# Attention and a rational-activation feed-forward on one core: new first loads, w_in laid out by chunk, and the weights' high parts rounded on GpSimd

## The chip, the cores and the metric

The kernel runs on 1 core of a Trainium2 chip. The metric is the device time of one execution in microseconds (us). Engines are named as the profile names them: PE (TensorE; PEld is its weight load), DVE (VectorE), ACT (ScalarE), POOL (GpSimd), SP (SyncE, which here only issues DMAs).

## The reference

Eight batches of eight heads, 576 positions of 64. Each head has a softmax attention over positions pooled by 4 and one over the 3 neighbours on either side; their sum is the input of a feed-forward layer with a rational function in the middle. The weights come as 64-bit floats (`float32 * (1.0 / np.sqrt(...))`).

```python
q_d, k_d, v_d = mean over groups of 4 positions of q, k, v
out_up    = np.repeat(sm_attn(q_d, k_d, v_d), 4, axis=2)
out_local = softmax(where(|i - j| < 4, q k^T / 8, -1e9)) @ v
x = (out_up + out_local).transpose(0, 2, 1, 3).reshape(4608, 512)

h = x @ w_in                       # 512 x 2048
P = a[0] + a[1] * h + a[2] * h**2 + a[3] * h**3
Q = 1.0 + abs(b[0]) * abs(h) + abs(b[1]) * h**2
return (P / (Q + 1e-06)) @ w_out   # 2048 x 512
```

## The kernel before

**Blocks.** The 4608 rows of x are worked in blocks of 512 rows (the first 512 positions of a batch), and in two blocks that hold the 64 remaining positions of four batches. The 2048 hidden columns are 16 chunks of 128 (`NFC`). For a block and a chunk, `h_part` makes h in PSUM, `middle` computes the rational function on ACT (four or five L710 operations per step) and DVE (L725 to L743, seven operations) into a high part `g` and a residue, and `o_part` (L762) multiplies with that chunk of w_out and adds up in four PSUM banks over all chunks. PE multiplies rounded pairs: high times high, low times high, high times low. In the first block alone `h_part` takes the unrounded weight and x in full precision (L685, two PE records per product) instead of the pairs (L697), so that the residues of w_in are needed only by the second block.

**Weights.** `weights(w, f, spot)` brings chunk f of w_in (w = 0) or w_out (w = 1) to SBUF. SP loads 512 KB of 64-bit words into a staging spot (L311 for w_in, L316 for w_out); ACT rescales the upper words (L325); DVE shifts them and puts the two words together as a 32-bit float `wb` (L328, L331). `parts` then rounds it to the high part `wh` (L345, on ACT) and subtracts for the residue `wl` (L348, on DVE). `wl` has the place of `wb`. The spots are called `st0` to `st4`, `sl0` to `sl3`, `sx0`, `sx1`; some lie in the room of later tiles. A load is 128 rows for w_out and 4 x 128 runs of 256 words for w_in, whose rows are 2048 columns long.

**Attention.** Work goes by pairs of heads, four pairs a batch, two pairs at a time. For a pair: `scores` (PE, L404 mask and L414), `softmax_local` (maximum on DVE, L446 and L453, exponentials on ACT, L461), the same for the pooled scores (`scores_pooled` L431, `softmax_pooled` L476 to L487), `normalize` (DVE L498 to L522), `turned` (transposes on PE, L535 and L542, copied back by ACT as `ept` and `et`, L548 to L559; the banks are its second argument), `weighted` (PE: the pooled part L584, which wants `vf` or `vp`, and the local part L573; ACT makes `up`, L630; DVE adds both into x, `xf`, L616). The pooled v of batch 0 is `vf`: one SP load (L816) and three accumulating DMAs that POOL issues (L820), each after the one before has landed. For later batches `pq` and `vp` are made likewise (L377 on SP, L381 on POOL).

**Order.** All instructions are first recorded as tasks with an engine, a cost and, for some, a due time. `Plan.run` goes through time and gives each free engine the ready task with the earliest latest-start; the result is a fixed order on each engine, and at run time the engines wait only for semaphores. A due time or a cost thus moves instructions. In the gaps of PE's planned order before the first block, products that nothing reads (`warm`, L898) are put in. Every engine works its order through one by one, so whatever waits holds up all that is behind it on that engine.

Of the kernel before, what the change touches and what calls it, by code (L numbers as in the profile page):

```python
# [9 lines left out]
F32 = mybir.dt.float32  # L10
# [9 lines left out]
DM, DF = 512, 2048  # L20
P = 128
NPAIR = H // 2
NCC = DM // P
NFC = DF // P
POOL = 4
# [51 lines left out]
class Plan:  # L77
# [11 lines left out]
    def add(self, engine, dur, fn, reads=(), writes=(), due=None, lag=None):  # L89
        t = Task()  # L90
        t.engine, t.dur, t.fn, t.due, t.n = engine, dur, fn, due, len(self.tasks)
        t.lag, t.preds, t.succs, t.late, t.start = lag, {}, [], 1e9, None
        rk = set().union(*(r.keys for r in reads)) if reads else set()
        wk = set().union(*(w.keys for w in writes)) if writes else set()
        for k in rk | wk:
            w = self.writer.get(k)
            if w is not None:
                t.preds[w] = True
        for k in wk:
            for r in self.readers.get(k, ()):  # L100
                t.preds.setdefault(r, False)
            self.writer[k] = t
            self.readers[k] = []
        for k in rk - wk:
            self.readers[k].append(t) if k in self.readers else self.readers.__setitem__(k, [t])
        t.preds.pop(t, None)
        for p in t.preds:
            p.succs.append(t)
        self.tasks.append(t)
        return t  # L110
# [57 lines left out]
def attention_moe(  # L168
# [12 lines left out]
    nc = tc.nc  # L181
# [3 lines left out]
    add = plan.add  # L185
# [5 lines left out]
    def put(name, shape, dtype, at=None):  # L191
        nonlocal top
        offset = top if at is None else at
        n = 2 if dtype == BF16 else 4
        for d in shape[1:]:
            n *= d
        if at is None:
            top = -(-(offset + n) // 32) * 32
        ap = nc.alloc_sbuf_tensor_at(name, shape, dtype, offset=offset).ap()
        room = Room(ap, (("S", k) for k in range(offset // 32, -(-(offset + n) // 32))))  # L200
        room.at = offset
        room.size = n
        return room
# [61 lines left out]
    vf = put("vf", [KC, NPAIR, 2, 2, D], F32, low[0][half].at)  # L265
# [30 lines left out]
    def setup_coef():  # L296
        add("SP", 0.1, lambda: nc.sync.dma_start(out=cf.ap[:, :6], in_=coef), (), (cf,), due=30.0)
        add("DVE", 0.1, lambda: nc.vector.memset(cone, CONE), (), (cf,))
        add(
            "ACT", 0.2, lambda: nc.scalar.activation(out=cf.ap[:, 4:6], in_=cf.ap[:, 4:6], func=AF.Abs),  # L300
            (cf,), (cf,),
        )


    def weights(w, f, spot, due=None):
        st = spot.ap.rearrange("p (c f two) -> p c f two", two=2, c=NCC)
        lo, word = low[w][f], bits[w][f]

        def load():
            if w == 0:  # L310
                nc.sync.dma_start(  # L311
                    out=st.rearrange("p c f two -> p c (f two)"),
                    in_=w_in[:, 2 * f * P : 2 * (f + 1) * P].rearrange("(c p) f -> p c f", p=P),
                )
            else:
                nc.sync.dma_start(  # L316
                    out=st.rearrange("p c f two -> p (c f two)"), in_=w_out[f * P : (f + 1) * P, :]
                )

        word1, word0 = st[:, :, :, 1], st[:, :, :, 0]  # L320

        def scaled():

            w1 = word1.bitcast(F32)
            nc.scalar.activation(out=w1, in_=w1, func=AF.Prelu, scale=2.0**-112, alpha=2.0**32)  # L325

        def upper():
            nc.vector.tensor_single_scalar(out=word.ap, in_=word1, scalar=3, op=ALU.logical_shift_left)  # L328

        def lower():  # L330
            nc.vector.scalar_tensor_tensor(  # L331
                out=word.ap, in0=word0, scalar=29, in1=word.ap,
                op0=ALU.logical_shift_right, op1=ALU.bitwise_or,
            )

        add("SP", 1.4, load, (), (spot,), due=due)
        add("ACT", 0.58, scaled, (spot,), (spot,))
        add("DVE", 0.335, upper, (spot,), (lo,))
        add("DVE", 0.6, lower, (spot, lo), (lo,))
        if w:  # L340
            parts(w, f)

    def parts(w, f, due=None):
        hi, lo, word = high[w][f], low[w][f], bits[w][f]
        add("ACT", 0.52, lambda: nc.scalar.copy(out=hi.ap, in_=word.ap.bitcast(F32)), (lo,), (hi,), due=due)  # L345
        add(
            "DVE", 0.6,
            lambda: nc.vector.tensor_tensor(  # L348
                out=lo.ap, in0=word.ap.bitcast(F32), in1=hi.ap.bitcast(F32), op=ALU.subtract
            ),  # L350
            (lo, hi), (lo,), due=due,
        )
# [12 lines left out]
    def load_qk(c, due=None):  # L365
        s, b, i = c.slot, c.b, c.i
        add("SP", 1.6, lambda: nc.sync.dma_start(out=s.qk.ap, in_=qk[b, i]), (), (s.qk,), due=due)

    def load_vw(c, due=None):
        s, b, i = c.slot, c.b, c.i  # L370
        add("SP", 0.9, lambda: nc.sync.dma_start(out=s.vw.ap, in_=vw[b, i]), (), (s.vw,), due=due)
# [156 lines left out]
    def turned(c, bk):  # L528

        s = c.slot  # L530
        tp, t0, t1 = bk

        def turn_pooled(kc, x):
            for i in range(NQ):
                nc.tensor.transpose(  # L535
                    out=x.ap[:KC, i * P : i * P + QR],
                    in_=s.ep.ap[:QR, i, kc * KC : (kc + 1) * KC],
                    identity=ident.ap[:QR, :QR],
                )

        def turn_local(k, dst):
            nc.tensor.transpose(  # L542
                out=dst, in_=s.el.ap[:, k].rearrange("p j k -> p (j k)"), identity=ident.ap
            )

        def keep_pooled(kc, x):
            src = x.ap[:KC, : NQ * P].rearrange("p (i j q) -> p (i j) q", j=2, q=D)
            nc.scalar.copy(  # L548
                out=s.ept.ap[:, kc].rearrange("p i j q -> p (i j) q"), in_=src[:, :, :QC]
            )  # L550

        add("PE", 0.31, lambda: turn_pooled(0, t0), (s.ep, ident), (t0,))
        add("PE", 0.31, lambda: turn_pooled(1, t1), (s.ep, ident), (t1,))
        add("ACT", 0.28, lambda: keep_pooled(0, t0), (t0,), (s.ept,))
        add("ACT", 0.28, lambda: keep_pooled(1, t1), (t1,), (s.ept,))
        add("PE", 0.44, lambda: [turn_local(k, tp.ap[:, k * P : (k + 1) * P]) for k in range(4)], (s.el, ident), (tp,))
        add("PE", 0.11, lambda: turn_local(4, t1.ap[:, NQ * P :]), (s.el, ident), (t1,))
        add("ACT", 0.49, lambda: nc.scalar.copy(out=s.et.ap[:, :4, :], in_=tp.ap.rearrange("p (c k) -> p c k", k=P)), (tp,), (s.et,))
        add("ACT", 0.16, lambda: nc.scalar.copy(out=s.et.ap[:, 4, :], in_=t1.ap[:, NQ * P :]), (t1,), (s.et,))  # L559
# [93 lines left out]
    def due_h(n):  # L653
        m = blocks[0].nstep
        return H0 + H_FIRST * min(n, m) + H_STEP * max(0, n - m)
# [148 lines left out]

    c0 = [Pair(p) for p in range(NPAIR)]
    due0 = due_h(0) - 4.0
    load_qk(c0[0], -19)
    load_qk(c0[1], -17)
    load_vw(c0[0], -14)
    load_vw(c0[1], -13)  # L810
    load_qk(c0[2], -11)
    load_qk(c0[3], -9)
    load_vw(c0[2], -7)
    load_vw(c0[3], -6)
    setup_coef()
    add("SP", 0.8, lambda: nc.sync.dma_start(out=vf.ap, in_=vp[0, 0]), (), (vf,), due=-15)  # L816
    for r in range(1, POOL):
        add(
            "POOL", 1.0,
            lambda r=r: nc.gpsimd.dma_start(out=vf.ap, in_=vp[0, r], accum_op=ALU.add),  # L820
            (vf,), (vf,), lag=4.0,
        )
    early = (-18.5, -16, -12, -10, -8, -5)
    for (w, f, spot), due in zip(chunks[: len(early)], early):
        weights(w, f, spot, due)
    bk = banks
    for q in range(2):
        cs = c0[2 * q : 2 * q + 2]
        for i, c in enumerate(cs):
            scores(c, bk[2 * i : 2 * i + 2])  # L830
            softmax_local(c, bk[2 * i : 2 * i + 2])
        for c in cs:
            pool_qk(c)
        sp = bk[4:6] if q == 0 else bk[0:2]
        scores_pooled(cs, sp)
        for c, y in zip(cs, sp):
            softmax_pooled(c, y)
        for i, c in enumerate(cs):
            normalize(c)
            turned(c, [bk[n] for n in ((6, 4, 5), (6, 4, 5), (6, 4, 5), (2, 0, 3))[2 * q + i]])  # L840
        weighted(cs, [bk[n] for n in ((4, 5, 4, 5), (0, 1, 4, 5))[q]], due0 - 10.0 * (1 - q))
    for w, f, spot in chunks[len(early) :]:
        weights(w, f, spot)

# [58 lines left out]
    for t in pe:  # L903
        n = int(WARM * (t.start - end) / 0.107)
# [85 lines left out]
```

## Time and profile before

| | |
|---|---|
| median of 3 runs | 988.06 us (987.84 to 988.74) |
| profiled execution | 987.5 us, span 985.7 us, granted clock 0.994 |
| PE busy | 961.4 us (98%), 7365 products |
| DVE busy | 839.4 us (85%) |
| ACT busy | 811.1 us (82%) |
| POOL busy | 148.1 us (15%) |
| DMA | 83.43 MB, mean 85 GB/s |
| chain that ended last | PE 85%, ACT 5%, DVE 4%, DMA 4% |

The span runs from the first to the last instruction. Busy shares are means over stages: in the first 56 us, when batch 0's attention is made and the first weights come, the DMA engines are near 100% and PE, DVE and ACT at two thirds; afterwards it is the reverse. The chain is followed from the last instruction back to whatever released it.

### The profile page before, as it was taken

To read this page: it belongs to the slowest core of one execution; us is meant where nothing else is said; L and a number is where in the kernel's file an instruction comes from. 1 tells how busy PE (TensorE), PEld (TensorE's weight loads), DVE (VectorE), ACT (ScalarE), POOL (GpSimd) and SP (SyncE) were. 2 spreads that over 40 slices of the span, in tenths; PEclk is the share of its full clock that TensorE was granted. 3 is DMA by queue.
4 is the path that set the end of the run, shared out by engine and by line. 5 is a ranking of instruction groups with operands and counts; after the bars stand their busy time and mean duration, and the time that the engine had idled before them with its cause. 6 is when DMAs were issued, how large, how long until landed. Compare 5 with 4: busy or idle time off the path is not lost.

```text
span 985.7 us, 19785 instructions
## 1 busy us (share of the span) xinstructions
PE 961.4 (98%) x7365; PEld 758.9 (77%) x7365; DVE 839.4 (85%) x1472; ACT 811.1 (82%) x2078; POOL 148.1 (15%) x177
## 2 busy tenths in 40 slices
PE   7789999999999999999999999999999999999997
PEld 5546666888888888988888887888878888898885
DVE  5789999988878978887978898888888888888886
ACT  5879988897979798679797978798887979767775
POOL 1300223122222212001212030303121220000000
PEclk9999999999999999999999999999999999999999
DMA  9983654333343234003335142524233320100001
GB/s 316 278 257 97 152 140 69 104 75 71 73 119 69 62 83 106 1 23 86 64 81 122 54 84 63 107 74 66 85 59 109 74 52 1 44 1 22 1 1 43
DMA packets 52515, 83.43 MB, mean 85 GB/s; under 512 B 6564, under 2 KB 37284, under 8 KB 52420
## 3 DMA queue, kind: packets, MB, share of 16 engines
q1 hardware_dynamic: 31972, 62.70, 19.5%
q0 software_dynamic: 20448, 19.48, 14.2%
q8 instruction: 58, 0.95, 0.4%
q14 instruction: 37, 0.30, 0.1%
HBM read 72.72 MB, written 9.44 MB: 83 GB/s over the span
## 4 chain that ended last, share of the span: by engine, by line
PE 85%; ACT 5%; DVE 4%; DMA 4%; issue 1%; SPq 0%; ACTq 0%; DVEq 0%
PE psum L762 37%; PE psum L697 36%; DMA vf<-in_vp_dram 3%; PE psum L573 2%; ACT m L710 2%; PE psum L584 2%; PE psum L542 2%; PE psum L535 1%; PE psum L414 1%; PE psum L685 1%; PE psum L431 1%; ACT gb L710 1%; DMA sx<-in_w_out_dram 1%; PE psum L404 1%; DVE wl L348 1%
## 5 line engine op out<-in xcount | busy, mean ns | idle before, releaser
L762 PE MATMUL psum<-wh,g 128*128 128x512 f32 x1152 | 369.8, 402 | 0.6 <-DVE g L743 0.4
L697 PE MATMUL psum<-xs,wh 128*128 128x512 f32 (+1 forms) x1152 | 265.1, 370 | 0.0
L710 ACT ACTIVATE m<-psum,cf 128x512 f32<-128x512 f32 x288 | 219.4, 767 | 39.2 <-PE psum L697 37.5
L762 PEld LDWEIGHTS psum<-wh,g 128*128 128x128 f32 x1152 | 208.6, 188 | 49.2 <-issue 4.8
L697 PEld LDWEIGHTS psum<-xs,wh 128*128 128x128 f32 x1152 | 199.3, 188 | 35.9
L762 PE MATMUL psum<-wl,g 128*128 128x512 f32 x576 | 224.7, 391 | 0.0
L710 ACT ACTIVATE gb<-psum,cf 128x512 f32<-128x512 f32 x144 | 116.5, 809 | 53.8 <-PE psum L762 53.8
L381 POOL DMA_DIRECT2D pq<-in_qkp_dram x84 | 73.8, 902 | 467.3 <-DMA pq<-in_qkp_dram 385.0
L697 PE MATMUL psum<-xs,wl 128*128 128x512 f32 (+1 forms) x576 | 141.6, 368 | 0.0
L734 DVE TENSOR_TENSOR g<-m,m 128x512 fp32r<-128x512 f32 x144 | 99.2, 689 | 44.0 <-ACT m L710 41.1
L725 DVE SCALAR_TENSOR_TENSOR m<-m,cf,m 128x512 f32<-128x512 f32 x144 | 107.6, 747 | 31.5 <-ACT m L710 31.4
L762 PEld LDWEIGHTS psum<-wl,g 128*128 128x128 f32 x576 | 108.1, 188 | 23.7
L461 ACT ACTIVATE el<-psum,nm 128x64 f32<-128x64 f32 x320 | 97.8, 352 | 28.4 <-DVE nm L453 28.4
L731 DVE TENSOR_TENSOR m<-m,gb 128x512 f32<-128x512 f32 x144 | 99.3, 690 | 20.7 <-ACT gb L710 16.5
L697 PEld LDWEIGHTS psum<-xs,wl 128*128 128x128 f32 x576 | 101.3, 189 | 19.0 <-issue 1.2
L710 ACT ACTIVATE gb<-m,cf 128x512 f32<-128x512 f32 x144 | 108.1, 751 | 0.0
L737 DVE SCALAR_TENSOR_TENSOR m<-m,g 128x512 f32<-128x512 f32 x144 | 99.3, 690 | 2.9
L742 DVE TENSOR_TENSOR m<-m,m 128x512 f32<-128x512 f32 x144 | 99.3, 690 | 2.9
L730 DVE TENSOR_TENSOR m<-m,m 128x512 f32<-128x512 f32 x144 | 98.6, 685 | 0.4 <-ACT m L710 0.4
L743 DVE TENSOR_TENSOR g<-m,m 128x512 fp32r<-128x512 f32 x144 | 98.0, 681 | 0.8
L710 ACT ACTIVATE m<-gb 128x512 f32<-128x512 f32 x144 | 94.7, 658 | 2.5
L381 POOL DMA_DIRECT2D vp<-in_vp_dram x84 | 71.1, 909 | 158.1 <-DMA vp<-in_vp_dram 156.2
(66 smaller groups left out, 990.6 us busy)
## 6 DMA issues: line engine op xcount, KB each, us to landing
qk<-in_qk_dram SPq DMA_DIRECT2D x32, 590.0 KB, 4.6
pq<-in_qkp_dram POOLq DMA_DIRECT2D x84, 144.0 KB, 3.3
vw<-in_vw_dram SPq DMA_DIRECT2D x32, 320.0 KB, 4.1
out_dram<-xf SPq DMA_DIRECT2D x32, 256.0 KB, 2.2
vp<-in_vp_dram POOLq DMA_DIRECT2D x84, 72.0 KB, 3.2
sl<-in_w_in_dram SPq DMA_DIRECT2D x10, 512.0 KB, 3.6
sl<-in_w_out_dram SPq DMA_DIRECT2D x10, 512.0 KB, 10.2
pq<-in_qkp_dram SPq DMA_DIRECT2D x28, 144.0 KB, 2.2
```

The costliest lines, as they stand in the source:

```text
L381: lambda d=dst, x=src, r=r: nc.gpsimd.dma_start(out=d.ap, in_=x[b, r, :, i], accum_op=ALU.add),
L461: nc.scalar.activation(out=s.el.ap[:, k, c.pos(j), :], in_=view[:, j, k, :], func=AF.Exp, bias=nm[:, 5 * j + k : 5 * j + k + 1], scale=sca ...
L697: nc.tensor.matmul(ph.ap[:, f * t : (f + 1) * t], lhsT=(high, low)[j][0][fc].ap[:, c, :], rhs=blk.x[i].ap[:, c, :], start=(part_ == 0 and ...
L710: add("ACT", cost, lambda: nc.scalar.activation(out=out_.ap, in_=in_, func=func, **kw), (room_in, cf, *more), (out_,))
L725: lambda: v.scalar_tensor_tensor(out=tb.ap, in0=tq.ap, scalar=b1, in1=tb.ap, op0=ALU.mult, op1=ALU.add),
L730: add("DVE", 0.61, lambda: v.tensor_tensor(out=ta.ap, in0=ta.ap, in1=tq.ap, op=ALU.mult), (ta, tq), (ta,))
L731: add("DVE", 0.61, lambda: v.tensor_tensor(out=ta.ap, in0=ta.ap, in1=u.ap, op=ALU.add), (ta, u), (ta,))
L734: add("DVE", 0.61, lambda: v.tensor_tensor(out=gh.ap, in0=ta.ap, in1=tq.ap, op=ALU.mult), (ta, tq), (gh,))
L737: lambda: v.scalar_tensor_tensor(out=tb.ap, in0=tb.ap, scalar=CONE, in1=gh.ap.bitcast(F32), op0=ALU.add, op1=ALU.mult),
L742: add("DVE", 0.61, lambda: v.tensor_tensor(out=tb.ap, in0=ta.ap, in1=tb.ap, op=ALU.subtract), (ta, tb), (tb,))
L743: add("DVE", 0.61, lambda: v.tensor_tensor(out=gl.ap, in0=tb.ap, in1=tq.ap, op=ALU.mult), (tb, tq), (gl,))
L762: nc.tensor.matmul(ob[sub].ap, lhsT=g[i].ap[:, f0 : f0 + P], rhs=flat((high, low)[j][1][fc].ap), start=(fc == 0 and m == 0), stop=(fc == N ...
```

## The change

Four things, in one diff:

1. The host lays w_in's words out by chunk, so that a chunk of w_in is 128 runs of 1024 words, like one of w_out; `load` has one form for both.
2. Batch 0's first loads come in another order, by new due times of `load_qk`, `load_vw`, `vf` and the first six chunks.
3. The PSUM banks of the transposes of pairs 2 and 3, and of their `weighted`, are others.
4. The high part `wh` is rounded by GpSimd, with a planned cost of 1.0 instead of 0.52.

```diff
@@ weights
         def load():
-            if w == 0:
-                nc.sync.dma_start(
-                    out=st.rearrange("p c f two -> p c (f two)"),
-                    in_=w_in[:, 2 * f * P : 2 * (f + 1) * P].rearrange("(c p) f -> p c f", p=P),
-                )
-            else:
-                nc.sync.dma_start(
-                    out=st.rearrange("p c f two -> p (c f two)"), in_=w_out[f * P : (f + 1) * P, :]
-                )
+            nc.sync.dma_start(
+                out=st.rearrange("p c f two -> p (c f two)"),
+                in_=w_in[f] if w == 0 else w_out[f * P : (f + 1) * P, :],
+            )
@@ parts
-        add("ACT", 0.52, lambda: nc.scalar.copy(out=hi.ap, in_=word.ap.bitcast(F32)), (lo,), (hi,), due=due)
+        add("POOL", 1.0, lambda: nc.gpsimd.tensor_copy(out=hi.ap, in_=word.ap.bitcast(F32)), (lo,), (hi,), due=due)
@@ batch 0
-    load_qk(c0[0], -19)
-    load_qk(c0[1], -17)
-    load_vw(c0[0], -14)
-    load_vw(c0[1], -13)
-    load_qk(c0[2], -11)
-    load_qk(c0[3], -9)
-    load_vw(c0[2], -7)
-    load_vw(c0[3], -6)
+    for c, due in zip(c0, (-19, -17, -15, -12)):
+        load_qk(c, due)
+    for c, due in zip(c0, (-14, -11, -8, -6)):
+        load_vw(c, due)
     setup_coef()
-    add("SP", 0.8, lambda: nc.sync.dma_start(out=vf.ap, in_=vp[0, 0]), (), (vf,), due=-15)
+    add("SP", 0.8, lambda: nc.sync.dma_start(out=vf.ap, in_=vp[0, 0]), (), (vf,), due=-18)
...
-    early = (-18.5, -16, -12, -10, -8, -5)
+    early = (-16, -13, -10, -9, -7, -5)
...
-            turned(c, [bk[n] for n in ((6, 4, 5), (6, 4, 5), (6, 4, 5), (2, 0, 3))[2 * q + i]])
-        weighted(cs, [bk[n] for n in ((4, 5, 4, 5), (0, 1, 4, 5))[q]], due0 - 10.0 * (1 - q))
+            turned(c, [bk[n] for n in ((6, 4, 5), (6, 4, 5), (2, 3, 0), (6, 1, 2))[2 * q + i]])
+        weighted(cs, [bk[n] for n in ((4, 5, 4, 5), (1, 2, 0, 3))[q]], due0 - 10.0 * (1 - q))
@@ kernel (host)
+    w_in = inputs["moe_w_in"].view(np.int64).reshape(NCC, P, NFC, P).transpose(2, 1, 0, 3).reshape(NFC, P, DM)
```

The lines of the kernel after stand 1 to 9 lower (L345 is L340 there, L685 is L680, L762 is L757, L898 is L889).

On SP, the first loads of the kernel before, from the mask's on (the number before the last one in a name is the pair, the spot or the chunk):

```order
L367 DMA qk0_193<-in_qk_dram 128x1180
L311 DMA st0_224<-in_w_in_dram 128x4x256
L367 DMA qk1_200<-in_qk_dram 128x1180
L311 DMA st1_225<-in_w_in_dram 128x4x256
L816 DMA vf_223<-in_vp_dram 72x1024
L371 DMA vw0_195<-in_vw_dram 128x640
L371 DMA vw1_202<-in_vw_dram 128x640
L311 DMA st2_226<-in_w_in_dram 128x4x256
L367 DMA qk2_209<-in_qk_dram 128x1180
```

And the same place of the kernel after:

```order
L362 DMA qk0_193<-in_qk_dram 128x1180
L807 DMA vf_223<-in_vp_dram 72x1024
L362 DMA qk1_200<-in_qk_dram 128x1180
L310 DMA st0_224<-in_w_in_dram 128x1024
L362 DMA qk2_209<-in_qk_dram 128x1180
L366 DMA vw0_195<-in_vw_dram 128x640
L310 DMA st1_225<-in_w_in_dram 128x1024
L362 DMA qk3_216<-in_qk_dram 128x1180
L366 DMA vw1_202<-in_vw_dram 128x640
```

`vf` has moved ahead of one pair's q and k and of two weight chunks; the weights stand behind the loads of the attention.

On ACT, the work of pairs 2 and 3 up to `up` in the kernel before (`ept`, `et`: transposed probabilities of the pooled and the local part; wh1_3 is chunk 3 of w_out):

```order
L345 CAST wh0_4_60<-wb0_4_97 128x512
L548 COPY ept2_214<-psum 72x288
L325 ACTIVATE sl1_230<-sl1_230 128x512
L548 COPY ept2_214<-psum 72x288
L325 ACTIVATE sl3_232<-sl3_232 128x512
L345 CAST wh1_3_75<-wb1_3_127 128x512
L558 COPY et2_213<-psum 128x512
L345 CAST wh1_4_76<-wb1_4_129 128x512
L559 COPY et2_213<-psum 128x128
L325 ACTIVATE sx1_234<-sx1_234 128x512
L630 ACTIVATE up0_191<-psum 128x144
```

The kernel after, from the same copy of `ept2` on:

```order
L543 COPY ept2_214<-psum 72x288
L320 ACTIVATE sx1_234<-sx1_234 128x512
L553 COPY et2_213<-psum 128x512
L554 COPY et2_213<-psum 128x128
L320 ACTIVATE sx0_233<-sx0_233 128x512
L543 COPY ept3_221<-psum 72x288 x2
L553 COPY et3_220<-psum 128x512
L554 COPY et3_220<-psum 128x128
L625 ACTIVATE up0_191<-psum 128x144
```

The casts are gone from between the copies, two rescalings are left there, and none stands right ahead of `up`; pair 3's copies have moved behind pair 2's.

On POOL, after the constants of the start, the kernel before has nothing but issues of accumulating DMAs. The kernel after has there:

```order
L811 DMA vf_223<-in_vp_dram 72x1024
L340 CAST wh0_0_56<-wb0_0_89 128x512
L811 DMA vf_223<-in_vp_dram 72x1024 x2
L340 CAST wh0_4_60<-wb0_4_97 128x512
L376 DMA pq0_194<-in_qkp_dram 128x288
L376 DMA pq1_201<-in_qkp_dram 128x288
L340 CAST wh0_1_57<-wb0_1_91 128x512
L376 DMA vp0_207<-in_vp_dram 72x256
L376 DMA pq0_194<-in_qkp_dram 128x288
L340 CAST wh1_0_72<-wb1_0_121 128x512
```

One cast has come between the first and the second accumulation of `vf`, and others between those of `pq` and `vp`, each of which waits for a landing.

More of the change, by code (lines that the diff above doesn't have):

```diff
@@ L969 @@
         "in_vp_dram": vpl,
-        "in_w_in_dram": inputs["moe_w_in"].view(np.int64),
+        "in_w_in_dram": w_in,
         "in_w_out_dram": inputs["moe_w_out"].view(np.int64),
```

## The prediction

> **What bounds the kernel now.** I read the table of stretches first, cut where TensorE (PE) starts the first block's products for good (55.8 us) and where the second block's first product stands (172.4 us). Its columns are busy time by engine, granted clock, mean DMA share, GB/s.
>
> ```profile
> core 0: us, PE busy (x) PEld busy (x) DVE busy (x) ACT busy (x) POOL busy (x), PEclk, DMA share, GB/s
> 0.00:55.80 55.80, 39.15 (x569) 27.66 (x569) 36.88 (x81) 37.71 (x151) 13.87 (x21) 0.94 1.00 302
> 55.80:172.40 116.60, 114.34 (x805) 69.86 (x805) 114.87 (x216) 106.38 (x276) 18.09 (x21) 0.99 0.50 132
> 172.40:985.70 813.30, 807.90 (x5998) 661.38 (x5992) 687.67 (x1177) 666.98 (x1652) 116.16 (x136) 1.00 0.27 63
> ```
>
> After 172.4 PE alone is the bound (807.90 of 813.30), and the change leaves its products there as they are. From 55.8 to 172.4 two engines are full at once: PE has 2.26 us left and VectorE (DVE) 1.73, ScalarE (ACT) 10.2. Only the first 55.8 us have slack, and there the DMA engines are full. So the change can gain before 55.8 and lose before 172.4. The chain of waits tells what the first stretch hangs on:
>
> ```profile
> 3.24 9.14 DMA vf<-in_vp_dram
> 12.69 7.79 DMA vf<-in_vp_dram
> 20.78 8.23 DMA vf<-in_vp_dram
> 29.29 7.84 DMA vf<-in_vp_dram
> 37.38 1.20 PE psum L584 x16
> ...
> 46.05 6.74 DMA sx<-in_w_out_dram
> ...
> 52.87 0.66 ACT sx L325
> ...
> 54.74 1.02 DVE xf L616 x4
> ```
>
> One load of `vf` and three accumulations on top of it, each waiting for the one before, end at 37.13; then comes the attention of the second two pairs, then a wait for a weight load on ACT. PE and ACT in time order (start, duration, in brackets the idle time and its releaser):
>
> ```profile
> 37.38 1.20 PE L584 MATMUL psum<-ept,vf 72*64 72x144 f32 x16 [2.53 <-DMA vf<-in_vp_dram]
> ...
> 43.99 1.04 PE L685 MATMUL psum<-xf,wb 128*128 128x512 f32 x2
> ...
> 45.16 2.75 PE L685 MATMUL psum<-xf,wb 128*128 128x512 f32 x6
> ...
> 50.63 0.71 PE L584 MATMUL psum<-ept,vf 72*64 72x144 f32 x8 [1.97 <-ACT et L559]
> 51.27 1.39 PE L573 MATMUL psum<-et,vw 64*64 64x58 f32 x80
> 55.81 5.39 PE L685 MATMUL psum<-xf,wb 128*128 128x512 f32 x8 [3.15 <-DVE xf L616]
> ```
>
> ```profile
> 42.09 3.21 ACT L345 CAST wh<-wb 128x512 fp32r<-128x512 f32 x6
> ...
> 47.88 0.69 ACT L325 ACTIVATE sl<-sl 128x512 f32<-128x512 f32 x1 [1.24 <-DMA sl<-in_w_out_dram]
> 48.47 0.60 ACT L345 CAST wh<-wb 128x512 fp32r<-128x512 f32 x1
> ...
> 52.87 0.65 ACT L325 ACTIVATE sx<-sx 128x512 f32<-128x512 f32 x1 [2.30 <-DMA sx<-in_w_out_dram]
> 53.43 0.45 ACT L630 ACTIVATE up<-psum 128x144 f32<-128x144 f32 x2
> ```
>
> PE's 1.97 and 3.15 us of idle time are both ACT's doing: it stands before weight loads (1.24 and 2.30 us) and casts while `et` and then `up` queue behind.
>
> **The change, step by step.** *First loads.* `vf` moves from sixth to third place on SP; st0, qk1 and st1 no longer stand ahead of it (512 + 590 + 512 KB, 1.65 MB). The rate at that time:
>
> ```profile
> 0.00:10.00 10.00, 5.76 (x72) 3.80 (x76) 4.29 (x9) 3.51 (x13) 0.70 (x6) 1.00 0.84 271
> 10.00:20.00 10.00, 8.04 (x146) 6.31 (x139) 6.92 (x14) 7.29 (x40) 0.99 (x1) 0.91 1.06 329
> ```
>
> 1.65 MB is 6.1 us at 271 GB/s and 5.0 at 329; I take 5.5. The accumulations took 7.8 to 8.2 us whatever was loading beside them, so all three move along, and the chain ends near 31.6. The scaled weights that moved behind are wanted later: their first use is the product at 43.99.
>
> *The cast in that chain.* On POOL the cast of wh0_0 now stands between the first and the second accumulation. It needs DVE's second word, which now follows the second pair's maximum:
>
> ```profile
> 12.12 0.17 DVE L453 TENSOR_TENSOR nm<-nm,scales 128x10 f32<-128x10 f32 x1
> ```
>
> 12.3 plus the two word operations (0.42 and 0.68 below) is 13.4, plus a cast of at most 0.9 gives 14.3; the first accumulation lands near 15 (12.4 - 5.5 + 0.3 + 7.8). Priced at nothing; the cover is under 1 us, and what is over it would delay both later accumulations.
>
> *Banks and PE order.* The stretch from 37.38 to 55.81 by PE's busy time: all of it, then L685 alone, then the warm-up products (L898) alone.
>
> ```profile
> 37.38:55.81 18.43, 13.31 (x225) 0.91 1.02 271
> 37.38:55.81 18.43, 3.79 (x9) 1.37 (x9) 0.91 1.02 271
> 37.38:55.81 18.43, 2.32 (x12) 1.41 (x12) 0.91 1.02 271
> ```
>
> 3.8 us go to the eight early L685 records (the ninth starts at the edge), 2.3 to twelve warm-ups, 7.2 to attention, 5.12 are idle. Afterwards the early L685 are gone from this place and 24 warm-ups stand in it: 7.2 + 24 x 0.193 = 11.8. To that I add a wait of 1.5 us, between 0 and the 3.15 seen before, because ACT still has sx1 and sx0 ahead of the last `et` and `up`. The first product that is not followed by a stall then comes 5.5 + 18.4 - 11.8 - 1.5 = 10.6 us earlier, near 45. Its queue order (half of chunks 1 and 0 first) covers the two last `xf` additions. The 3.8 us of L685 are still to do: PE gains 10.6 - 3.8 = 6.8.
>
> *Layout of w_in.* 512 pieces of 1 KB a load become 128 of 4 KB, which is how w_out is loaded. The views of the two lines, L311 (w_in) and then L316 (w_out), end with:
>
> ```profile
> DMA to landing us min/median/max: 3.6/6.3/13.6
> DMA to landing us min/median/max: 4.3/8.9/11.9
> ```
>
> Least loaded, the old form lands 0.7 us sooner, not later; at most (under accumulations) 1.7 us later. Per load it is between +0.7 and -1.7, and it is hidden: of 16 such loads ACT waits on few. Taken as zero; with the cover gone for two of them, +1.4 to -3.4.
>
> *Casts leave ACT.* The window up to 172.4 with the cast's line (L345) alone:
>
> ```profile
> 0.00:172.40 172.40, 20.01 (x32) 0.97 0.66 187
> ```
>
> 32 casts of 0.63 us leave ACT, but ACT isn't what is full in 55.8 to 172.4, and PE has only 2.26 us to win there. Zero beyond the waits above.
>
> *DVE.* By PE's first lasting product DVE had finished the words of w_out chunks 3, 4 and 12 and two residues; now these come behind it.
>
> ```profile
> L348 DVE TENSOR_TENSOR wl<-wb,wh 128x512 fp32r<-128x512 f32 x20 | 13.6, 684 | 0.0
> ...
> L331 DVE SCALAR_TENSOR_TENSOR wb<-sl,wb 128x512 int32<-128x512 int32 x15 | 10.1, 684 | 0.0
> L328 DVE TENSOR_SCALAR wb<-sl 128x512 int32<-128x512 int32 x15 | 6.1, 419 | 0.5 <-ACT sl L325 0.5
> ```
>
> These means overlap by some 0.08 us, so 3 x (0.34 + 0.60) + 2 x 0.60 = 4.0. DVE is full, so its stretch begins 10.6 earlier and lasts 4.0 longer: 6.6 gained, a little less than PE's 6.8. DVE sets the end.
>
> *Casts come to GpSimd (POOL).* 6 of the 32 stand before the first lasting product, 26 behind it, all where DVE is 98.5% busy. No row has a POOL instruction that reads as much beside DVE. For the length, the set-up instructions; for DVE beside a busy POOL, the residue line L743 (columns: window, DVE busy, count) without POOL and with 12 issues of POOL:
>
> ```profile
> masks.py:199 POOL TENSOR_SCALAR_AFFINE_SELECT ident<-ident 128x128 f32<-128x128 f32 x1 | 0.3, 289 | 0.1
> masks.py:197 POOL MEMSET ident<- 128x128 f32 x1 | 0.2, 206 | 0.3 <-POOLq L975 0.3
> ...
> L975 POOL MEMSET const-float32-1.0<- 128x1 f32 x1 | 0.1, 100 | 0.0
> ```
>
> ```profile
> 60.00:100.00 40.00, 4.09 (x6) 1.00 0.41 133
> 106.00:134.00 28.00, 2.74 (x4) 1.00 0.57 118
> ```
>
> For four times the columns a cast is 0.53 (by MEMSET) to 0.86 us (by AFFINE_SELECT). POOL has room: 26 x 0.86 + 18.09 is 40 us of 117. L743 is 0.68 us in both windows, so POOL's issues took nothing from DVE. That is the nearest row, and I take 0 per cast. The other end is that DVE stands for as long as the cast streams, 0.43 to 0.76 us: 11 to 20 us in 26 casts. Less than nothing is excluded, as DVE keeps all its instructions.
> The Trainium skill speaks against my end ("SBUF — State Buffer", section "Who interferes with whom"): a VectorE instruction with two SBUF inputs uses the read port that GpSimd has too, and whichever comes second waits. No run here shows it, since POOL's DMA issues are no such reads. By it the sum would be a loss, the first rival below.
>
> **Sum.** -5.5 for `vf`, -5.1 for the stretch behind it, +4.0 for DVE's postponed work, 0 for the casts: -6.6 against the profiled execution's 987.5 (span 985.7 and 1.8 around it), so 980.9. The median of the runs, 988.06, is 0.56 above that execution: 981.5.
>
> **Rivals.** *DVE pays for the casts.* One mechanism: in 45 to 165 us each cast holds up a two-input DVE operation, and DVE has nothing to give. At s us per cast the time is 981.5 + 26 s; it is slower than before from s = 0.25 (6.6 / 26). At 0.43 it is 993, at 0.63 (the cast on ACT) 998. For it: DVE's fullness, and that nearly all of its operations there read two SBUF operands (m,m; wb,wh). Against it: L743. Where some casts fall beside reductions or PSUM reads, about 994. Chance 0.34.
> *The early gain is eaten by the next wait.* ACT's scaling of st1 to sx0 stands ahead of `et` and `up` in a fixed order, and the DMA engines are full. If ACT waits there as it did (1.24 + 2.30) and the cast delays the accumulations by 1 us, 981.5 + 4.5 = 986, up to 988. For it: DMA share 1.00; against it: 1.65 MB less ahead of `vf`. Chance 0.15.
> *The change does not shorten the chain at all* (the accumulations start as late as before, since they share full DMA engines): PE then keeps only 5.1 - 3.8 = 1.3 us, about 986.8; counted in the 0.15.
>
> **How the numbers follow.** The forecast has 0.51: 981.5, by itself 977 to 986 (a second `et` wait saved or 1.5 us lost, both ends of the rate). A measurement of this kernel tells about 0.2%, 2 us, from no change. Faster by more: 0.51 and little else, 0.51; within 2 us: most of the second rival, 0.13; slower: the first rival and the tail of the second, 0.36. The range runs from 977 to 997, where about 0.06 lies below (an `et` stall less and the DMA lighter) and 0.13 above (s over 0.6).
>
> **What would show it.** `vf` landing near 7, its chain ending at 31 to 32; L680 without a stall from 43 to 47; the second block's first product at 165 to 166. Right on the casts: DVE's two-input operations still 0.68 us; wrong: 1.1 us and more for some of them, with PE idle for DVE in 60 to 165 us. A chain that still ends near 37, or ACT waiting over 3 us for weight loads in 25 to 42 us, would make the second rival true.

## The result and the profile after

The changed kernel takes 994.43 us (median of 4 runs, 994.15 to 995.14). The kernel before took 988.4 us on the same chip, so the ratio is 1.0051 (95% interval 1.0032 to 1.0071): slower by half a per cent. The profiled execution's span is 992.7 us, 7.0 more than before.

Where the time went shows in a table of stretches, cut at 57.7 us (the rational function of the first block begins on DVE) and where the second block's first product stands. Columns are length, busy time by engine, granted clock, DMA share, GB/s. First the kernel before:

```profile
57.70:172.40 114.70, 112.45 (x804) 69.00 (x802) 112.97 (x213) 105.06 (x273) 18.09 (x21) 0.99 0.49 128
```

Then the kernel after:

```profile
0.00:57.70 57.70, 41.71 (x621) 28.25 (x621) 41.15 (x85) 34.40 (x144) 17.54 (x27) 0.97 0.97 306
57.70:178.56 120.86, 110.64 (x709) 67.84 (x709) 118.61 (x207) 95.99 (x251) 46.21 (x46) 0.99 0.46 121
178.56:992.70 814.14, 808.67 (x6037) 661.99 (x6035) 689.31 (x1181) 666.20 (x1652) 116.65 (x136) 1.00 0.27 63
```

The last stretch is 0.8 us longer than before (814.14 against 813.30). The rest of the loss lies ahead of the second block, whose first product comes at 178.56 instead of 172.40. There DVE is full (118.61 of 120.86), and it is busy 5.6 us longer than before with 6 instructions fewer.

Its groups from 50 to 175 us say which ones got longer (line, operation, count, then busy us, mean ns, idle before):

```profile
L343 DVE TENSOR_TENSOR wl<-wb,wh 128x512 fp32r<-128x512 f32 x20 | 15.3, 763 | 1.5 <-POOL wh L340 1.5
L726 DVE TENSOR_TENSOR m<-m,gb 128x512 f32<-128x512 f32 x16 | 13.4, 837 | 0.0
L720 DVE SCALAR_TENSOR_TENSOR m<-m,cf,m 128x512 f32<-128x512 f32 x16 | 13.3, 829 | 0.4 <-ACT m L705 0.4
L729 DVE TENSOR_TENSOR g<-m,m 128x512 fp32r<-128x512 f32 x15 | 11.6, 772 | 0.0
...
L737 DVE TENSOR_TENSOR m<-m,m 128x512 f32<-128x512 f32 x15 | 10.2, 678 | 0.0
```

In the same window of the kernel before (five line numbers higher there) L726 took 686 ns, L720 746, L729 681, L343 684. A mean of 837 hides a few long ones. They stand in time order beside the casts; first GpSimd (POOL), then DVE:

```profile
42.31 0.98 POOL L340 CAST wh<-wb 128x512 fp32r<-128x512 f32 x1
...
59.11 3.23 POOL L340 CAST wh<-wb 128x512 fp32r<-128x512 f32 x5
...
85.72 4.46 POOL L340 CAST wh<-wb 128x512 fp32r<-128x512 f32 x3 [10.30 <-DVE wb L326]
```

```profile
42.50 1.07 DVE L323 TENSOR_SCALAR wb<-sx 128x512 int32<-128x512 int32 x1
...
59.72 3.17 DVE L726 TENSOR_TENSOR m<-m,gb 128x512 f32<-128x512 f32 x1
...
88.65 1.06 DVE L343 TENSOR_TENSOR wl<-wb,wh 128x512 fp32r<-128x512 f32 x1 [0.51 <-POOL wh L340]
89.64 1.09 DVE L732 SCALAR_TENSOR_TENSOR m<-m,g 128x512 f32<-128x512 f32 x1
```

Five casts run back to back from 59.11 to 62.34, and the multiplication that started at 59.72 ends at 62.89: it stood until all of them were through. One cast alone makes a 0.68 us operation 1.09. It goes the other way too: from 85.58 DVE has two shifts and three two-input operations one behind the other, and three casts take 4.46 us instead of some 1.8 (three times 0.61). The chain of waits now holds both kinds:

```profile
59.72 3.17 DVE m L726
85.72 2.90 POOL wh L340
115.97 3.16 POOL wh L340
150.56 2.83 POOL wh L340
```

The start of the kernel did become quicker. POOL's three accumulations of `vf` (start, duration, idle before) and PE's first products:

```profile
7.88 0.98 POOL L811 DMA_DIRECT2D vf<-in_vp_dram  x1 [6.58 <-DMA vf<-in_vp_dram]
12.54 0.60 POOL L340 CAST wh<-wb 128x512 fp32r<-128x512 f32 x1 [3.67 <-DVE wb L326]
16.68 0.83 POOL L811 DMA_DIRECT2D vf<-in_vp_dram  x1 [3.55 <-DMA vf<-in_vp_dram]
24.73 0.83 POOL L811 DMA_DIRECT2D vf<-in_vp_dram  x1 [7.21 <-DMA vf<-in_vp_dram]
```

```profile
32.48 1.20 PE L579 MATMUL psum<-ept,vf 72*64 72x144 f32 x16
...
47.03 8.80 PE L680 MATMUL psum<-xf,wb 128*128 128x512 f32 x16 [3.89 <-DVE xf L611]
...
59.06 7.23 PE L680 MATMUL psum<-xf,wb 128*128 128x512 f32 x16 [2.38 <-ACT gb L705]
```

The last accumulation goes out at 24.73 (29.29 before), and the product that waited for it no longer waits; the first lasting h product stands at 47.03 instead of 55.81, 8.8 us earlier, though PE waits 3.89 us for `xf` before it and 2.38 for ACT's rational function soon after.

### The profile page after: what moved, and what is told of

The parts are those of the page before. It is cut to its first block, busy times and chain, and to the rows that moved or that the text cites. A ratio compares the mean times of both kernels' runs of the same rounds, so it can differ in the third digit from the quotient of the medians.

```text
span 992.7 us, 19799 instructions
## 1 busy us (share of the span) xinstructions
PE 961.0 (97%) x7365; PEld 758.1 (76%) x7365; DVE 849.1 (86%) x1472; ACT 796.6 (80%) x2046; POOL 180.4 (18%) x209
## 4 chain that ended last, share of the span: by engine, by line
PE 82%; DVE 10%; DMA 4%; issue 2%; POOL 1%; SPq 1%; ACT 1%; ACTq 0%; DVEq 0%; POOLq 0%
PE psum L757 36%; PE psum L692 36%; PE psum L568 2%; DMA pq<-in_qkp_dram 2%; PE psum L579 1%; PE psum L530 1%; PE psum L537 1%; PE psum L409 1%; PE psum L426 1%; DMA qk<-in_qk_dram 1%; DVE m L720 1%; DMA sx<-in_w_out_dram 1%; DVE m L726 1%; POOL wh L340 1%; DVE g L729 1%
## 5 line engine op out<-in xcount | busy, mean ns | idle before, releaser
L757 PE MATMUL psum<-wh,g 128*128 128x512 f32 x1152 | 371.7, 403 | 4.7 <-DVE g L738 2.7
L757 PEld LDWEIGHTS psum<-wh,g 128*128 128x128 f32 x1152 | 209.3, 188 | 55.5 <-issue 7.7
L757 PE MATMUL psum<-wl,g 128*128 128x512 f32 x576 | 225.0, 392 | 0.0
L729 DVE TENSOR_TENSOR g<-m,m 128x512 fp32r<-128x512 f32 x144 | 100.6, 699 | 43.2 <-ACT m L705 41.3
L720 DVE SCALAR_TENSOR_TENSOR m<-m,cf,m 128x512 f32<-128x512 f32 x144 | 108.9, 756 | 31.2 <-ACT m L705 31.1
L757 PEld LDWEIGHTS psum<-wl,g 128*128 128x128 f32 x576 | 108.4, 188 | 23.4
L726 DVE TENSOR_TENSOR m<-m,gb 128x512 f32<-128x512 f32 x144 | 101.7, 706 | 20.3 <-ACT gb L705 16.3
```

What stands on the lines that cost most here:

```text
L720: lambda: v.scalar_tensor_tensor(out=tb.ap, in0=tq.ap, scalar=b1, in1=tb.ap, op0=ALU.mult, op1=ALU.add),
L726: add("DVE", 0.61, lambda: v.tensor_tensor(out=ta.ap, in0=ta.ap, in1=u.ap, op=ALU.add), (ta, u), (ta,))
L729: add("DVE", 0.61, lambda: v.tensor_tensor(out=gh.ap, in0=ta.ap, in1=tq.ap, op=ALU.mult), (ta, tq), (gh,))
L757: nc.tensor.matmul(ob[sub].ap, lhsT=g[i].ap[:, f0 : f0 + P], rhs=flat((high, low)[j][1][fc].ap), start=(fc == 0 and m == 0), stop=(fc == N ...
```

## The experiments

Three theories were on trial. The port (A): a cast on GpSimd and a VectorE operation that reads SBUF twice exclude each other, and DVE pays. The queue (B): the casts stand behind POOL's accumulating DMAs, each of which waits for a landing, and DVE waits for late casts. The loads (C): the new first loads and banks themselves lost time.

**Casts back on ACT.** The changed kernel with one line as before:

```diff
-        add("POOL", 1.0, lambda: nc.gpsimd.tensor_copy(out=hi.ap, in_=word.ap.bitcast(F32)), (lo,), (hi,), due=due)
+        add("ACT", 0.52, lambda: nc.scalar.copy(out=hi.ap, in_=word.ap.bitcast(F32)), (lo,), (hi,), due=due)
```

> The changed kernel with the cast of the high parts back on ACT at its old planned cost; new loads, banks and w_in layout stay. Theory A (a GpSimd instruction that reads SBUF and a DVE operation with two SBUF operands keep each other out): the loss goes with the casts, and the 5 us that the first stretch gains stay, 980 to 984 us. Theory B (the casts stand behind POOL's waits for landings, and what needs them is late): the same, 980 to 984. Theory C (the new order of loads and banks is itself at fault): 990 us or more.

Measured 985.69 us (7 runs), ratio 0.996 [0.9945, 0.9975]: faster than both kernels. C falls. The casts on GpSimd cost the changed kernel 0.9% (1.0051 against 0.996), and the rest of the change gains 0.4%, less than A and B expected (980 to 984). Its table:

```profile
57.70:169.20 111.50, 108.17 (x752) 67.04 (x752) 109.97 (x207) 103.43 (x271) 17.79 (x21) 1.00 0.47 126
```

Against the changed kernel this stretch is 9.36 us shorter. DVE has 207 instructions in both and is busy 8.64 us less (109.97, 118.61); its idle time makes up 0.72. The polynomial begins at nearly the same time in both (57.93 and 57.70), so the loss of the changed kernel lies behind that point.

**The cast alone.** The kernel before with nothing but the casts on GpSimd (the opposite edit, in the other kernel):

> The kernel before with the cast moved to GpSimd at planned cost 1.0 and nothing else. Theory A: 8 to 12 us slower than before, 996 to 1000, since here the first stretch gains nothing, and two-input DVE operations of up to 3 us. Theory B: 991 to 994. Theory C: 987 to 989, within what can be told from no change.

996.72 us (4 runs), ratio 1.006 [1.0037, 1.0084]: A's time. 16 two-input operations of 128x512 on DVE are lengthened to 0.95 us or more up to the second block, the longest to 1.6 and not to the 3 that A allowed, and the second block begins at 181.71 instead of 172.40 (in the slowest of the four runs, the one profiled). The loss needs none of the other edits.

**ACT's plan, GpSimd's cast; and without the reads.** To keep the order of PE, DVE and SP, the task is planned as ACT's and issued on GpSimd. In the second kernel GpSimd fills the tile and reads one column of the word:

```diff
+        add("ACT", 0.52, lambda: nc.gpsimd.tensor_copy(out=hi.ap, in_=word.ap.bitcast(F32)), (lo,), (hi,), due=due)
...
+        def write_only():
+            nc.gpsimd.tensor_copy(out=hi.ap[:, 0, :1], in_=word.ap[:, 0, :1].bitcast(F32))
+            nc.gpsimd.memset(hi.ap.bitcast(F32), 0.0)
+        add("ACT", 0.52, write_only, (lo,), (hi,), due=due)
```

> As the run with the cast on ACT, planned with it there, so that PE, DVE and SP have the same order, but issued on GpSimd: only the engine of the cast differs. Theory A: 8 us or more above the run with the cast on ACT, and the means of the two-input DVE operations L720, L726, L729 above 0.75 us in the first 180 us. Theory B: 2 to 5 us above it, with those means at 0.68 to 0.75 and more waits of DVE for wh. Theory C: no difference, within 2 us.

> As the run before it, but instead of the cast GpSimd copies one column (so that it waits for the same word) and then fills the high part with zeros: it is as busy and in the same place of its queue, but reads next to nothing from SBUF. The weights' high parts are zero, so the output is another. Theory A: the time falls back to that of the cast on ACT, within 2 us, and DVE's operations to 0.68 us. Theory B: no better than the run with the real cast, within 2 us.

997.84 us (6 runs), 1.0082 [1.0064, 1.0101], and 992.68 us (10 runs), 1.0025 [1.0011, 1.0038]. The first is A's time, though of the three means that A named only L720's is above 0.75 us (0.84; L726 0.68, L729 0.70): which operations meet a cast changes with the order. The second is neither theory's: without the reads no two-input operation of DVE is long any more, but the time does not fall back to 985.69. DVE's waits in the second kernel (us in total, times, longest) say why:

```profile
DVE wl L347 <- POOL wh L342: 11.4, 6, 4.8
```

So a queue cost exists as well where casts stand at places meant for ACT: behind accumulations that wait. This pair does not tell the shares in the changed kernel, whose plan knows that the casts are POOL's, and where DVE waits 3.8 us for them in all. The spare casts further below do.

**Three casts out of the queue.** The changed kernel with the casts of w_out's chunks 0 to 2, which stood behind the accumulations of `pq`, on ACT:

```diff
+        if w == 1 and f < 3:
+            add("ACT", 0.52, lambda: nc.scalar.copy(out=hi.ap, in_=word.ap.bitcast(F32)), (lo,), (hi,), due=due)
+        else:
             add("POOL", 1.0, lambda: nc.gpsimd.tensor_copy(out=hi.ap, in_=word.ap.bitcast(F32)), (lo,), (hi,), due=due)
```

> The changed kernel with the casts of w_out's chunks 0 to 2 on ACT (cost 0.52 in the plan, as before) and the other 29 on GpSimd. These three stand behind GpSimd's accumulating loads of q and k in the first 50 us. If the queue is half of the loss, the first product of the second block comes 3 to 5 us earlier (173.5 to 175.5 against 178.56) and the time falls to a ratio of 1.000 to 1.002 against the kernel before. If the excluded reads of SBUF are all of it, three casts of 32 are worth 3 x 0.25 = 0.8 us: a ratio of 1.004 to 1.005 and the first product near 177.8.

995.88 us (6 runs), 1.0069 [1.0047, 1.009]: not faster at all. B's number fails, and A's too: the second block begins at 180.57, not near 177.8. What B said of the place came true, since PE no longer waits for `xf`:

```profile
44.84 7.11 PE L683 MATMUL psum<-xf,wb 128*128 128x512 f32 x16
...
58.50 6.39 PE L683 MATMUL psum<-xf,wb 128*128 128x512 f32 x8 [5.71 <-ACT gb L708]
```

The 2.2 us won are lost at the next wait. In the new order DVE begins the rational function at 61.34 instead of 57.70, with held weight work ahead of it (two words in 3.02 us, a residue in 2.17 after a wait of 1.75 for its cast), and from 57.70 up to the second block it is busy 121.31 of 122.87 us. Since the order has changed with the edit, this run does not tell the queue's share; the next pair keeps the order.

**Casts that nobody waits for.** The kernel with casts on ACT, the order of the other four engines row for row the same, and beside it a second cast of each finished high part on GpSimd, into a tile that nobody reads; then the same with a fill in place of the cast:

```diff
+        add("POOL", 0.05, lambda: nc.gpsimd.tensor_copy(out=spare.ap, in_=hi.ap.bitcast(F32)), (hi,), ())
...
+        def write_only():
+            nc.gpsimd.tensor_copy(out=spare.ap[:, 0, :1], in_=hi.ap[:, 0, :1].bitcast(F32))
+            nc.gpsimd.memset(spare.ap.bitcast(F32), 0.0)
+        add("POOL", 0.05, write_only, (hi,), ())
```

> The version with all but the casts on GpSimd (casts on ACT, the order of PE, VectorE, ACT and SyncE row for row that of the 985.69 us run), and beside it a second cast of each of the 32 high parts on GpSimd, from the finished high part into a tile that nobody reads. No engine waits for these casts. If excluded reads of SBUF are the loss, VectorE is busy some 8 us longer before the second block (32 x 0.25 us) and the time is that of the changed kernel: first product of the second block at 176 to 178.5, ratio 1.002 to 1.006. If waiting for GpSimd's queue is the loss, this is the 985.69 us kernel again: first product at 169 to 170, ratio 0.995 to 0.998.

> As the run with the spare casts, but GpSimd copies one column of the high part and fills the tile that nobody reads with zeros: as long on GpSimd, nearly no reads. With excluded reads as the cause: no VectorE operation of 128x512 longer than 0.75 us beyond those on the cast line's one column, first product of the second block at 169 to 170, ratio 0.995 to 0.998. If GpSimd's work or its writes by themselves cost something (accumulating loads issued later, write traffic), the time goes up here as with the spare casts: ratio 1.002 or more.

994.19 us (6 runs), 1.0041 [1.0025, 1.0056], and 986.29 us (7 runs), 0.9962 [0.9948, 0.9976], on the same chip. The tables of the two:

```profile
57.70:178.87 121.17, 113.20 (x753) 68.67 (x753) 120.52 (x210) 105.74 (x272) 50.40 (x46) 0.97 0.45 119
```

```profile
57.70:169.57 111.87, 108.32 (x753) 67.02 (x753) 110.69 (x208) 103.56 (x271) 55.24 (x71) 1.00 0.47 126
```

This settles it. Casts whose result is thrown away cost what the real ones cost: DVE is busy 9.8 us longer, and the second block begins 9.3 us later, as between the changed kernel and its casts on ACT (9.36), so little is left there for the queue. With no queue to wait in and no data to wait for, only the shared time of the two engines is left. The granted clock differs as well (0.97 and 1.00), but it isn't what sets the end: with the spare casts PE has 7.97 us left in this stretch and DVE 0.65. A fill takes 0.55 us in the mean, about as long as an undisturbed cast (0.56 to 0.61), and the fills cost nothing, so it is the reads. That POOL is busier still with the fills (55.24 us against 50.40) is due to the one-column casts ahead of them: each reads SBUF, and they stand behind DVE's two-input operations (0.89 us in the mean), the longest here:

```profile
79.69 4.90 POOL L344 CAST spare<-wh 128x1 fp32r<-128x1 f32 x1
```

One group of DVE with the spare casts, and its like with the fills:

```profile
L327 DVE SCALAR_TENSOR_TENSOR wb<-sl,wb 128x512 int32<-128x512 int32 x16 | 12.9, 812 | 0.0
```

```profile
L327 DVE SCALAR_TENSOR_TENSOR wb<-sl,wb 128x512 int32<-128x512 int32 x16 | 10.8, 682 | 0.0
```

The Trainium skill says just this ("SBUF — State Buffer", section "Who interferes with whom"): a VectorE instruction with two SBUF inputs contends with a GpSimd instruction that reads SBUF, not with one that only writes it. These two runs agree.

**Half the casts.** The condition of the three casts as `w == 1`, so that ACT rounds w_out and GpSimd w_in:

> The changed kernel with the 16 casts of w_out on ACT and the 16 of w_in on GpSimd. With excluded reads as the cause the loss goes with the number of casts: half of 9.4 us, first product of the second block at 173 to 175, ratio 1.000 to 1.002. With GpSimd's queue as the cause nearly all of the loss goes, since the casts that stood behind the accumulating loads in the first 50 us were those of w_out (but one or two): first product near 170, ratio 0.996 to 0.998.

988.91 us (12 runs), 0.9987 [0.9975, 0.9999]. DVE is busy 114.42 of 115.12 us up to the second block at 172.82. From 0 casts to 16 to 32 the second block begins at 169.20, 172.82, 178.56. That is a little under A's numbers (173 to 175, ratio 1.000 to 1.002) and over B's (near 170, 0.996 to 0.998). The loss goes with the number of casts: 10 of these 16 start after 57.70, against 24 of the 32, and 3.6 of 9.4 us is near that share.

**The other two parts of the change, each alone.** First loads, bases and banks with the casts on ACT and w_in as before; then the layout of w_in alone.

> The kernel before with the new first loads, the new bases and the new banks alone: w_in keeps its layout, the casts stay on ACT. If the early part carries the gain that the version with all but the casts showed (985.69 against 989.52, 3.8 us), this comes to about the same, a ratio of 0.995 to 0.998, with the first product of the second block near 169. If the layout of w_in carries it, the time stays with the kernel before (ratio 0.999 to 1.001) and the first product of the second block stands near 172.

> The kernel before with w_in's words laid out by chunk and nothing else. The prediction's step priced this at 0: a ratio of 0.999 to 1.001, first product of the second block within 0.5 us of 172.4. The rival that gives the layout the gain of the version without the casts on GpSimd expects 0.996.

988.18 us, 0.999 [0.9979, 1.0002], and 990.03 us, 1.0011 [0.9998, 1.0023] (12 runs each); neither can be told from the kernel before. The first is what the layout's theory expects and the second denies that theory, so neither part carries the 0.4% by itself: only together do they gain. ACT shows where; that it is the whole reason was not tried. Its order puts the rescalings of the last early weight loads ahead of the first operation of the rational function. With both parts, then with the loads and banks alone:

```profile
52.24 0.67 ACT L320 ACTIVATE sl<-sl 128x512 f32<-128x512 f32 x1 [1.40 <-DMA sl<-in_w_in_dram]
...
56.15 0.69 ACT L320 ACTIVATE sl<-sl 128x512 f32<-128x512 f32 x1 [1.13 <-DMA sl<-in_w_out_dram]
56.75 0.67 ACT L705 ACTIVATE m<-psum,cf 128x512 f32<-128x512 f32 x1
```

```profile
53.62 0.67 ACT L325 ACTIVATE sl<-sl 128x512 f32<-128x512 f32 x1 [1.67 <-DMA sl<-in_w_in_dram]
...
57.98 0.72 ACT L325 ACTIVATE sl<-sl 128x512 f32<-128x512 f32 x1 [0.48 <-DMA sl<-in_w_out_dram]
58.55 0.72 ACT L710 ACTIVATE m<-psum,cf 128x512 f32<-128x512 f32 x1
```

The new form of the w_in loads brings that function 1.8 us forward, and the second block begins at 169.20 instead of 172.04; in the kernel before the function began at 59.52. With the layout alone it began at 61.41 and the second block at 176.18, not within 0.5 us of 172.4 as expected, though the profiled execution (991.27 us) was the slowest of the twelve: `vf` still landed late, and the clock granted from 30 to 50 us was 0.83 instead of 0.91. Whether that clock goes with the layout was not tried.

**The two engines by themselves.** A kernel of five stages that does nothing else, in a single run:

> Not the attention kernel: 16 VectorE two-input additions of 128x512 f32 alone, 16 GpSimd casts of 128x512 f32 to fp32r alone, 16 of each together, 16 one-input reduces with 16 casts, 16 two-input additions with 16 GpSimd memsets; the output is not the reference's. If the two engines exclude each other on reads of SBUF, additions and casts together take about the sum of both (0.68 + 0.61, near 1.3 us for each pair), while the reduces and the memsets leave the times of the pieces alone. If the lengthened additions of the changed kernel come from something else in it (its DMAs, its PSUM traffic), the additions keep 0.68 in all three mixes and a pair takes as long as the slower of its two.

In time order (start, duration of the whole row):

```profile
4.39 9.72 DVE L40 TENSOR_TENSOR d<-a,b 128x512 f32<-128x512 f32 x16 [4.39 <-DMA b<-in_x_dram]
...
14.73 10.11 POOL L46 CAST hi<-word 128x512 fp32r<-128x512 f32 x18
23.19 2.18 DVE L40 TENSOR_TENSOR d<-hi,b 128x512 f32<-128x512 f32 x1 [9.08 <-POOL hi L46]
25.30 14.47 DVE L40 TENSOR_TENSOR d<-a,b 128x512 f32<-128x512 f32 x15
25.44 13.19 POOL L46 CAST hi<-word 128x512 fp32r<-128x512 f32 x13 [0.60 <-DVE d L40]
...
41.11 8.99 POOL L46 CAST hi<-word 128x512 fp32r<-128x512 f32 x16
...
52.49 10.13 DVE L40 TENSOR_TENSOR d<-a,b 128x512 f32<-128x512 f32 x16
```

An addition takes 0.61 us alone (9.72 / 16), 0.96 beside casts (14.47 / 15) and 0.63 beside fills (10.13 / 16). A cast takes 0.56 alone (10.11 / 18), 1.01 beside additions (13.19 / 13) and 0.56 beside reductions (8.99 / 16). A pair together takes about 1.0 us, not the full sum of 1.17 (0.61 + 0.56) and less than the 1.3 expected: the exclusion is nearly whole, but some 0.2 us of each pair does overlap. In these mixed stages no DMA moves and PE does nothing, so the long operations need neither.

## Why the prediction was wrong

The sign was wrong: it said 981.5 us and gave the first rival, "DVE pays for the casts" ("about 994"), 0.34. That rival came true in its mechanism. That its time fits as well (994.43 measured) is partly luck: it put 12.5 us for the casts on a base of 981.5, while the casts cost 8.7 us (994.43 against 985.69) on a base of 985.69.

- *Casts come to GpSimd (POOL)* is the step that failed. It took 0 per cast from L743, which stayed at 0.68 us beside POOL's DMA issues. Those issues are no reads of SBUF like a cast's, as the step itself said, so the nearest row was the wrong kind. With the casts, DVE is busy 8.64 us longer from 57.70 on than without them: 0.36 for each of the 24 casts that run there, above the break-even of 0.25 that the rival had named and below its 0.43 to 0.76. A cast that meets a two-input operation by itself costs 0.41 us (1.09 - 0.68), and not every cast meets one. By the second block's first product, which came at 178.56 and not at the forecast's 165.8 (172.4 - 6.6), 9.4 of the 12.8 us are this step (178.56 against 169.20), and 3.4 the next one.
- *Banks and PE order* was right in mechanism and too large. The first lasting product came 8.8 us earlier, not 10.6, and it kept little of that: with the casts on ACT, where nothing else disturbs, the second block begins 3.2 us earlier (169.20), not 6.6. "Its queue order covers the two last `xf` additions" failed: those additions stand behind weight work on DVE, and PE waits 3.89 us for them (2.46 with the casts on ACT). Then the step followed PE only up to its first product. The rational function comes next, and ACT has weight rescalings ahead of it that wait for full DMA engines: it began at 56.75 instead of 59.52. That is the second rival, "the early gain is eaten by the next wait", one stage later than it was looked for, and with 3.4 of its 4.5 us.
- *First loads* was right: the last accumulation lands at 24.73 + 7.3 = 32.0 instead of 37.13, 5.1 us earlier against 5.5.
- *The cast in that chain* was right at nothing: it is over at 13.14, and the second accumulation waits for the first one's landing until 16.68.
- *Layout of w_in* at zero holds for the layout alone, but not beside the new loads, where 1.8 us of the gain hang on it. "ACT waits on few" of those loads was true, and one of the few stood ahead of the rational function.
- *Casts leave ACT*: zero was right, as ACT was not what was full.
- *DVE*, 4.0 us of postponed work, did not come. With the casts on ACT DVE is busy 150.3 us up to the second block, before it was 151.8, in 294 instructions against 296: nothing had to be made up for.

Of the signs listed, those for "wrong" were right: two-input operations of 1.1 us and more, and PE idle for DVE (2.6 us for `g` after 57.7, 0.3 before).

## What to carry to other kernels

Before moving work to an idle engine, ask what else that engine shares with the full one: the price of a GpSimd cast was not on GpSimd but on VectorE, and it was settled by casts whose results nobody reads, with fills as a control. A row of the nearest kind is no evidence when it lacks the very property that costs (here, reading SBUF). And a gain in an early stage has to be followed to the first operation of the next stage on every engine; here two parts of the change were worth nothing apart and 0.4% together, most likely because a late weight load stood in front of it. The version to keep has the other three parts of the change, with the casts left on ACT: 985.69 us.

## What the runs showed of the hardware

- Exclusion holds in both directions: one multiplication stood 3.17 us under five casts, and a single cast took up to 3.16 us while VectorE worked back to back (115.97 in the chain). The Trainium skill ("SBUF — State Buffer", section "Summary: rules for kernel authors") says that the second one to issue "fully blocks" until the first finishes. These rows agree that it blocks, but what waited stood for longer than the one instruction that was first: for five casts one way, for five VectorE operations the other way (from 85.72), and for nine in the case of the one-column cast at 79.69. In the five-stage kernel the two took turns, and 0.2 us of a pair overlapped. What decides between turns and runs was not tried.
- A one-input operation of DVE was held as well: the shift L323 took 1.07 us beside a cast (42.50), 0.42 without. A fill, which only writes, held such a shift too, as these rows of the run with the spare fills show (0.68 us):

```profile
56.98 0.53 POOL L345 MEMSET spare<- 128x512 f32 x1
57.11 0.68 DVE L324 TENSOR_SCALAR wb<-sl 128x512 int32<-128x512 int32 x1 [0.23 <-ACT sl L321]
```

- Two-input operations were not held by fills: none of 128x512 took over 0.76 us up to the second block. Reductions and casts left each other alone: 16 casts took 8.99 us beside them (0.56 each, as alone), and the reductions 0.69 us each, beside the casts and after them.
